# The sum over tokens with x held and k moved in 64 columns, and VectorE keeping x in plain rows

## The chip, the cores and the metric

One core of one Trainium2 chip. The metric is the device time of one execution in microseconds. TensorE (PE) multiplies, VectorE (DVE), ScalarE (ACT) and GpSimd (POOL) work element by element, SyncE (SP) issues DMAs. PEld is the loading of the operand that PE holds (the "stationary" one), which overlaps the matmuls.

## What is computed

Eight batches of 3200 tokens: a gated attention without softmax, whose result `x` goes through a token mixer.

```python
scores = (1 / S) * (z @ z.T)              # S = 3200, z is S x 64
x      = u * (maximum(scores, 0)**2 @ v)  # u, v, x are S x 256
wq, wk = x @ w_q, x @ w_k                 # S x 64
mixed  = (1 / 8) * (wq @ wk.T) @ x        # S x 256
out    = maximum(mixed, 0) @ w_out
```

The kernel never forms `wq @ wk.T`. It forms the sum over tokens `wk.T @ x`, a matrix of 64 x 256 for each batch (called heads), and multiplies `wq` with that (called mix).

## The kernel before

**Tiles and stages.** The 3200 tokens of a batch are 25 blocks of 128, in 7 groups: six of 512 tokens and a last one of 128 (`LASTG`). For each group, PE forms the scores of 128 x 512 tokens at a time (`scores`, tile `sc`, two at once as a pair on the upper and the lower 64 rows), DVE or ACT clips and scales them out of PSUM (`first_stage`, tile `g`), POOL or ACT squares them (`second_stage`, tile `at`), and some are turned by DMA for use in another group (`tt`, `ttl`). The product with `v` is accumulated in four PSUM banks (`second_product`, tiles `acc`): two halves of a group, each in two banks, one for the upper and one for the lower 64 rows of a block. All these matmuls come in pairs on the two halves of the rows, 64 rows by 128 columns.

**Behind each half of a group** (`gate`): ACT copies one bank out, DVE adds the other (tile `both`, line L369; with that the two banks are free again), and POOL multiplies by `u` and writes `x_sb` in fp16 (L388). `x_sb` is laid out in an interleaved way, so that one DMA transpose (`turn_x`) gives `xT_sb`.

**The mixer for a group.** `projections` (L417) gives q and k of the group from `xT_sb`; ACT copies them out (`qk`), a DMA transpose gives k with tokens on the partitions (`kx`, `turn_keys`), with 64 columns of k in one half of each block's 128 columns. `double_keys` (L447, POOL) copies these 64 columns into the other half, so that the 128 columns of the held operand hold k twice. `heads` (L454) then holds the doubled k (128 columns) and moves `x_sb` (256 columns), a pair for each block of 128 tokens; its result has `wk.T @ x` twice, on the upper and the lower 64 partitions, since `mix` needs it on both. `heads_out` (L467, L469, DVE) adds it to `ha`, 512 columns for the two banks, and after the last group POOL adds the two parts of `ha` to `hs` (L476). Then `mix` (L482), ACT's clip (L503), the product with `w_out` (`proj`, L513), its scaling out of PSUM by DVE or ACT (L535, L540, tile `fo` in SBUF, two buffers) and the store (L541) follow for each group of the batch.

**PSUM.** Four banks belong to `acc`. The other four are two buffers of two banks, `ps_tile`, which `sc`, `qk`, `hd`, `mx` and `fo` share in turn: a matmul into one of them waits until what stood there two tiles before has been copied out.

**Order.** The order of each engine is written out by a list scheduler in the kernel's own text. It keeps a clock for each engine (`give(engine, ready, weight)`), a list of timed calls (`at_time`), of extras that are fitted in between (`add_extra`: keys, heads, mix, proj) and of DMAs with due times (`move`), which SP issues. Engines then run in that order and wait for each other by semaphores.

**The last batch** differs: for its last three groups the sum over tokens is formed by `last_gram` and `last_heads` from a second copy of x (`xd`, L377), and the mixes stand at the end of the program, outside the scheduler.

Of the kernel before, what the change touches and what calls it, by code (L numbers as in the profile page):

```python
# [9 lines left out]
FP16 = mybir.dt.float16  # L10
# [6 lines left out]
def kernel(  # L17
# [32 lines left out]
    FINAL_SCALE = 1.0 / (8.0 * ALPHA * ALPHA * ALPHA)  # L50

    NAT = 16
    NX = 7
    NXT = 4
    NEARBY = 8
    KEEP = 4
# [3 lines left out]
    pzt = ctx.enter_context(tc.tile_pool(name="pzt", bufs=2))  # L60
    pv = ctx.enter_context(tc.tile_pool(name="pv", bufs=2))
    px = ctx.enter_context(tc.tile_pool(name="px", bufs=NX))
    pk = ctx.enter_context(tc.tile_pool(name="pk", bufs=3))
    pxt = ctx.enter_context(tc.tile_pool(name="pxt", bufs=NXT))
    pu = ctx.enter_context(tc.tile_pool(name="pu", bufs=2))
# [17 lines left out]
    def top(r):  # L83
        return slice(r * dqk, (r + 1) * dqk)

    ctx.enter_context(tc.manual_schedule())

    zT, vs, us, xs, xTs, qks, ks, hacc, hss, rts = ({} for _ in range(10))

    def rows(t, b):  # L90
        return t[b].rearrange("(p n) d -> p n d", n=NT)
# [242 lines left out]

    accs, xds = {}, {}

    def weights(b, gi, ti, j):
        if (b, gi, ti) in made:  # L340
# [20 lines left out]

    def gate(b, gi, half):
        if (b, gi) not in xs:
            assert len(xs) < NX, (b, gi, list(xs))
# [3 lines left out]
        nc.scalar.copy(out=both[:, 0 : n * D], in_=accs[half, 0][:, 0 : n * D])  # L368
        nc.vector.tensor_add(  # L369
            out=both[:, 0 : n * D], in0=accs[half, 1][:, 0 : n * D], in1=both[:, 0 : n * D]  # L370
        )
        if b == last and gi >= LASTG - 2:
            if gi == LASTG - 2 and half == 0:
                spare = pv.tile([P, NT, D], FP16, tag="v_sb", name="xd")
                for i in range(3):
                    xds[LASTG - 2 + i] = spare[:, 4 * i : min(4 * i + 4, 9), :]
            nc.vector.tensor_mul(  # L377
                out=xds[gi][:, 2 * half : 2 * half + n, :].rearrange("p n d -> p (n d)"),
                in0=both[:, 0 : n * D],
                in1=us[b, gi][:, 2 * half : 2 * half + n, :].rearrange("p n d -> p (n d)"),  # L380
            )
        u_rows = us[b, gi][:, 2 * half : 2 * half + n, :].rearrange("p n (c d) -> p (n c) d", d=dh)
        if 2 * half + n == widths[gi] // P:
            us.pop((b, gi))

        def make_x():
            for r in [half] if widths[gi] == W else range(2):
                nc.gpsimd.tensor_mul(  # L388
                    out=xs[b, gi][:, 0:n, :, r, :].rearrange("p n c d -> p (n c) d"),
                    in0=both[:, 0 : n * D].rearrange("p (m d) -> p m d", d=dh),  # L390
                    in1=u_rows,
                )

        make_x()

    def turn_x(b, gi):
# [8 lines left out]
    def x_rows(b, gi, n):  # L405
        return xs[b, gi][:, n % 2, :, n // 2, :]

    def halves(gi):  # L410
        return range((widths[gi] // P + 1) // 2)
# [30 lines left out]
    def double_keys(b, gi):  # L442
        doubled.add((b, gi))
        nn = widths[gi] // P
        for r in halves(gi):
            sl = slice(2 * r, min(2 * r + 2, nn))
            nc.gpsimd.tensor_copy(out=ks[b, gi][:, sl, r, :], in_=ks[b, gi][:, sl, 1 - r, :])  # L447

    def heads(b, gi, ps, begun=()):
        nn = widths[gi] // P  # L450
        assert (b, gi) in doubled
        for n in range(nn):
            for r in range(2):
                nc.tensor.matmul(  # L454
                    out=ps[:, r, D : 2 * D],
                    lhsT=ks[b, gi][top(r), n, :, :].rearrange("p a h -> p (a h)"),
                    rhs=x_rows(b, gi, n)[top(r), :, :],
                    start=(n == 0 and r not in begun),
                    stop=(n == nn - 1),
                )  # L460
        del xs[b, gi]

    def heads_out(b, gi, ps):
        part = ps[:, 0:2, D : 2 * D]
        if gi == 0:
            hacc[b] = psml.tile([P, 2, D], FP32, tag="ha", name="ha")
            nc.vector.tensor_copy(out=hacc[b][:], in_=part)  # L467
        else:
            nc.vector.tensor_add(out=hacc[b][:], in0=part, in1=hacc[b][:])  # L469
        if gi == LASTG:  # L470
            heads_done(b)

    def heads_done(b):
        hss[b] = psml.tile([P, D], FP16, tag="hs", name="hs")
        ha = hacc.pop(b)
        nc.gpsimd.tensor_add(out=hss[b][:], in0=ha[:, 0, :], in1=ha[:, 1, :])  # L476

    def mix(b, gi, banks):
        n = min(2, widths[gi] // P)
# [120 lines left out]
    def at_time(t, fn):  # L600
        later.append((t, fn))
# [14 lines left out]
    def add_extra(t, kind, fn):  # L616
        extras.append((t, kind, fn))
        extras.sort(key=lambda x: x[0])
# [18 lines left out]
    def close_slot(t):  # L637
        slots.append(t)
# [65 lines left out]
                row_at[b, gj, starts[gi] // P + n] = t + 0.5  # L704

    def double(b, gi):
        keys_at[b, gi] = give(POOL, clock[PE], 0.6) + 0.5
        double_keys(b, gi)

    def use_keys(b, gi):  # L710
        open_slot()
        ps = ps_tile("qk")
        prior = None
        if keyed and keys_at.get(keyed[0], 1e9) <= clock[PE]:
            prior = keyed.pop(0)
        projections(b, gi, ps, stop=not prior)
        clock[PE] += 0.44 if gi < LASTG else 0.24
        if prior:
            heads(*prior, ps, halves(gi))
            clock[PE] += 0.44 if prior[1] < LASTG else 0.11  # L720
        ready = clock[PE] + FROM_PE
        projections_out(b, gi, ps)
        done = give(ACT, ready, 0.56)
        n = widths[gi] / P
        final = (b, gi) == (last, LASTG - 2)
        if not final:
            move(
                done + SLACK, done + 10.0, 1.28, 0.21 * n, lambda: turn_keys(b, gi),
                lambda t: at_time(t, lambda: double(b, gi)),
            )  # L730
            keyed.append((b, gi))
        if prior:
            heads_out(*prior, ps)
            done = give(DVE, done, 0.7)
            if prior[1] == LASTG:
                give(POOL, done, 0.6)
                heads_known(prior[0])
        close_slot(done)
        if len(keyed) == 2 and gi == LASTG:
            add_extra(done + 14.0, "heads", use_heads)  # L740
        if final:
            for _ in keyed[1:]:
                add_extra(done, "heads", use_heads)

    def use_heads():
        open_slot()
        ps = ps_tile("hd")
        prior = keyed.pop(0)
        heads(*prior, ps)
        clock[PE] += 0.44 if prior[1] < LASTG else 0.11  # L750
        heads_out(*prior, ps)
        done = give(DVE, clock[PE] + FROM_PE, 0.7)
        if prior[1] == LASTG:
            give(POOL, done, 0.6)
            heads_known(prior[0])
        close_slot(done)

    def heads_known(b):
        t = clock[PE]
        for i, gis in enumerate(([0, 1], [2, 3, LASTG], [4, 5])):  # L760
            for gi in gis:
                add_extra(t + 4.0 + (MIXES if b < last - 1 else MIXES_END) * i, "mix", lambda gi=gi: use_mix(b, gi))

    def use_mix(b, gi):
        open_slot()
# [275 lines left out]
    while extras or later or moves:  # L1041
# [17 lines left out]
        else:  # L1059
            extras.remove(x)  # L1060
            x[2]()
    assert not pending and len(keyed) == 1
    def mixed(b, gi, i=None):
        if i is None:
            ps = ps_tile("mx")
# [22 lines left out]
    use_heads()  # L1088
# [57 lines left out]
```

## Time and profile before

| | |
|---|---|
| times of three runs | 780.02, 780.99, 781.06 us (median 780.99) |
| profiled execution | span 780.0 us |
| PE busy | 98% of the span, 12410 matmuls |
| PEld, DVE, ACT, POOL busy | 86%, 63%, 72%, 79% |
| TensorE clock granted | full in nearly every slice |
| DMA | 141 MB, 181 GB/s in the mean |

Busy time is the time in which an engine had an instruction of its own under way. A row of instructions gives line, engine, operation, what it writes and reads, the shape and the count, then busy time in us and the mean of one in ns, then the idle time before them and what ended it. A row of a timeline gives start and length in us; rows of the same kind next to each other are put together. Since matmuls overlap in the pipeline, the length of one (269 ns) is more than the distance from one to the next.

### The profile page before, as it was taken

The page shows a single profiled execution, that of the slowest core. Times are in us where ns is not written, and L with a number is a line of the kernel's source. Part 1 is how long each engine was busy: PE and PEld are TensorE (multiplying, and loading weights), DVE is VectorE, ACT ScalarE, POOL GpSimd, SP SyncE. Part 2 cuts the span into 40 slices and gives each one's busy share as a digit, 9 for nine tenths or more (in the row PEclk, how much of TensorE's full clock was granted, in tenths as well). Part 3 has the DMA queues.
Part 4 walks back from the last instruction along what each step waited for, and adds up shares of the span by engine and source line. Part 5 has one row for each costly group of instructions (what it writes and reads, how often), then busy time and mean ns, then how long its engine had stood idle before and what let it go on. Part 6 is the DMA issues. An engine that isn't in the chain of part 4 may idle for free.

```text
span 780.0 us, 28286 instructions
## 1 busy us (share of the span) xinstructions
PE 765.9 (98%) x12410; PEld 674.0 (86%) x12410; DVE 490.5 (63%) x506; ACT 558.1 (72%) x672; POOL 619.5 (79%) x518
## 2 busy tenths in 40 slices
PE   8999999999999999999999999999999999999996
PEld 6889989988888888988889888898888988999894
DVE  6576768767565766655657556575566765656534
ACT  6786785676877776876678777787778578777644
POOL 7798887668986978887779769887888868887850
PEclk9999999999999999999999999999999999999999
DMA  7899999999999999999899999999989999989725
GB/s 181 157 152 175 162 160 170 171 187 180 222 183 190 200 218 204 151 170 217 198 171 193 168 221 168 199 161 171 241 159 208 162 196 211 157 169 168 183 81 198
DMA packets 307116, 141.11 MB, mean 181 GB/s; under 512 B 285744, under 2 KB 288432, under 8 KB 306992
## 3 DMA queue, kind: packets, MB, share of 16 engines
q1 hardware_dynamic: 300224, 123.13, 85.8%
q0 software_dynamic: 6624, 15.98, 14.6%
q8 instruction: 97, 1.59, 0.9%
q14 instruction: 27, 0.22, 0.1%
q10 hardware_dynamic: 144, 0.20, 0.1%
HBM read 59.64 MB, written 26.21 MB: 110 GB/s over the span
## 4 chain that ended last, share of the span: by engine, by line
PE 94%; DVE 2%; DMA 1%; ACT 1%; issue 1%; POOL 0%; DVEq 0%; SPq 0%
PE acc L352 68%; PE sc L265 13%; PE fo L513 6%; PE qk L417 3%; PE qk L454 2%; PE mx L482 1%; DVE g L291 1%; DMA v_sb<-in_v_dram 1%; ACT g L287 1%; DVE both L369 0%; DVE fo L535 0%; DMA z<-in_z_dram 0%; ACT at L307 0%; PE xtx L555 0%; PE hd L454 0%
## 5 line engine op out<-in xcount | busy, mean ns | idle before, releaser
L352 PE MATMUL acc<-v_sb,at 64*128 64x256 f16 x7344 | 506.0, 269 | 2.3 <-issue 1.5
L309 POOL TENSOR_TENSOR at<-g 128x1024 f16<-128x1024 f32 (+2 forms) x240 | 432.5, 1813 | 88.0 <-DVE g L291 46.8
L352 PEld LDWEIGHTS <-at 64*128 64x128 f16 x7344 | 403.9, 94 | 54.5 <-issue 9.7
L291 DVE TENSOR_SCALAR g<-sc 128x1024 f32<-128x1024 f32 (+2 forms) x302 | 349.9, 1175 | 121.8 <-PE sc L265 109.8
L307 ACT ACTIVATE at<-g 128x1024 f16<-128x1024 f32 (+2 forms) x242 | 241.6, 1015 | 25.0 <-DVE g L291 22.5
L287 ACT ACTIVATE g<-sc 128x1024 f32<-128x1024 f32 (+2 forms) x177 | 174.8, 990 | 56.2 <-PE sc L265 50.9
L265 PE MATMUL sc<-zT 64*128 64x512 f16 x924 | 185.3, 375 | 2.4 <-DVE g L291 1.2
L388 POOL TENSOR_TENSOR x_sb<-both,u_sb 128x512 f16<-128x512 f32 (+1 forms) x112 | 134.3, 1205 | 48.9 <-DVE both L369 48.4
L352 PE MATMUL acc<-v_sb,tt 64*128 64x256 f16 x2272 | 168.0, 269 | 0.0
L352 PEld LDWEIGHTS <-tt 64*128 64x128 f16 x2272 | 127.0, 94 | 10.3 <-issue 0.6
L369 DVE TENSOR_TENSOR both<-acc,both 128x512 f32<-128x512 f32 (+1 forms) x104 | 69.5, 670 | 70.9 <-ACT both L368 62.0
L368 ACT COPY both<-acc 128x512 f32<-128x512 f32 (+1 forms) x104 | 58.9, 566 | 66.5 <-PE acc L352 63.1
L265 PEld LDWEIGHTS <-zT 64*128 64x128 f16 x924 | 62.2, 94 | 9.8 <-issue 5.2
L535 DVE TENSOR_SCALAR fo<-fo 128x1024 f32<-128x1024 f32 (+2 forms) x31 | 32.7, 1067 | 41.4 <-PE fo L513 41.3
L503 ACT ACTIVATE rt<-mx 128x1024 f16<-128x1024 f32 (+1 forms) x49 | 45.5, 931 | 12.2 <-PE mx L482 12.0
L430 ACT CAST qk<-qk 128x512 f16<-128x512 f32 (+1 forms) x54 | 29.4, 544 | 29.2 <-PE qk L454 25.4
L513 PE MATMUL fo<-wo,rt 128*128 128x256 f16 x400 | 49.4, 273 | 0.1
L469 DVE TENSOR_TENSOR ha<-qk,ha 128x512 f32<-128x512 f32 x37 | 25.6, 691 | 36.1 <-ACT qk L430 35.8
L513 PEld LDWEIGHTS <-rt 128*128 128x128 f16 x400 | 36.4, 98 | 10.8 <-issue 6.5
L540 ACT ACTIVATE fo<-fo 128x1024 f32<-128x1024 f32 (+2 forms) x27 | 24.6, 914 | 19.8 <-PE fo L513 19.8
L417 PE MATMUL qk<-xT_sb,wqk 64*128 64x256 f16 (+1 forms) x404 | 32.2, 265 | 0.0
L454 PE MATMUL qk<-x_sb,kx 64*128 64x256 f16 x360 | 29.1, 269 | 0.0
(44 smaller groups left out, 237.0 us busy)
## 6 DMA issues: line engine op xcount, KB each, us to landing
u_sb<-in_u_dram SPq DMA_DIRECT2D x48, 512.0 KB, 5.0
out_dram<-fo SPq DMA_DIRECT2D x46, 512.0 KB, 4.4
v_sb<-in_v_dram POOLq DMA_DIRECT2D x35, 320.0 KB, 6.2
zn<-in_z_dram POOLq DMA_DIRECT2D x7, 400.0 KB, 6.3
tt<-at SPq DMA_TRANSPOSE x143, 4.5
u_sb<-in_u_dram SPq DMA_DIRECT2D x8, 128.0 KB, 3.6
out_dram<-fo SPq DMA_DIRECT2D x8, 128.0 KB, 3.5
out_dram<-fo SPq DMA_DIRECT2D x4, 256.0 KB, 4.2
```

The costliest lines, as they stand in the source:

```text
L265: nc.tensor.matmul(out=sc[:, h, 0:gw], lhsT=z_cols(b, h, ti * P, P), rhs=z_cols(b, h, gs, gw), start=True, stop=True,)
L287: nc.scalar.activation(out=g[:, hs, 0:w], in_=sc[:, hs, 0:w], func=RELU, scale=GSCALE)
L291: nc.vector.tensor_scalar(out=g[:, hs, 0:w], in0=sc[:, hs, 0:w], scalar1=0.0, scalar2=GSCALE, op0=AOP.max, op1=AOP.mult,)
L307: nc.scalar.square(out=out, in_=g[:, hs, 0:w])
L309: nc.gpsimd.tensor_mul(out=out, in0=g[:, hs, 0:w], in1=g[:, hs, 0:w])
L352: nc.tensor.matmul(out=accs[half, r][:, ds((j % 2) * D, D)], lhsT=weights(b, gi, ti, j)[top(r), :], rhs=vs[b][top(r), ti, :], start=(first ...
L368: nc.scalar.copy(out=both[:, 0 : n * D], in_=accs[half, 0][:, 0 : n * D])
L369: nc.vector.tensor_add(out=both[:, 0 : n * D], in0=accs[half, 1][:, 0 : n * D], in1=both[:, 0 : n * D])
L388: nc.gpsimd.tensor_mul(out=xs[b, gi][:, 0:n, :, r, :].rearrange("p n c d -> p (n c) d"), in0=both[:, 0 : n * D].rearrange("p (m d) -> p m ...
L417: nc.tensor.matmul(out=ps[:, r, 0 : n * P], lhsT=wqk[top(r), c, :, :].rearrange("p t h -> p (t h)"), rhs=xTs[b, gi][top(r), 0:n, c, :], st ...
L503: nc.scalar.activation(out=out, in_=ps[:, 0:nr, 0 : ND * n * P], func=RELU)
L513: nc.tensor.matmul(out=banks[r][:, ds(j * D, D)], lhsT=flat[:, ds((dc * n + j) * P, P)], rhs=wo[:, dc, :], start=(dc == 0 and j == 0), sto ...
```

## The change

For all batches but the last, `heads` changes the two operands' places: x is held (128 of its 256 columns at a time, so twice as many matmuls) and the 64 columns of k are moved. k need not be doubled then. The result is the transposed sum, 128 partitions by 2 x 64 columns for each of two banks. `ha` has half the columns; POOL adds its two parts twice, into the two halves of a new tile `ht`, and a DMA transpose (`turn_heads`) gives `hs` in the layout that `mix` has always had. The mixes of a batch become known to the scheduler when that DMA should have landed.

A held operand must have its columns side by side. DVE therefore copies `x_sb` into a tile `xn` with plain rows (`keep_x`), once for each half of a group, after POOL has written it; the last batch's last three groups have no such copy. `x_sb` has 3 buffers in place of 7, and `xn` has 5. The last batch keeps the old operands (with `xn` moved in place of `x_sb`), and its `ha` lies in one of the two SBUF buffers with the tag `fo`.

```diff
@@ gate: after x_sb is made @@
+    def keep_x(b, gi, half):
+        if (b, gi) not in xns:
+            xns[b, gi] = pxn.tile([P, 4, D], FP16, tag="xn", name="xn")
+        n = min(2, widths[gi] // P - 2 * half)
+        nc.vector.tensor_copy(
+            out=xns[b, gi][:, 2 * half : 2 * half + n, :].rearrange("p n (c d) -> p n c d", d=dh),
+            in_=xs[b, gi][:, 0:n, :, half, :],
+        )
@@ heads @@
-        assert (b, gi) in doubled
+        x = xns.pop((b, gi))
         for n in range(nn):
-            for r in range(2):
-                nc.tensor.matmul(
-                    out=ps[:, r, D : 2 * D],
-                    lhsT=ks[b, gi][top(r), n, :, :].rearrange("p a h -> p (a h)"),
-                    rhs=x_rows(b, gi, n)[top(r), :, :],
...
+            if b == last:
+                todo = [(D, D, ks[b, gi][:, n, :, :].rearrange("p a h -> p (a h)"), x[:, n, :])]
+            else:
+                k = ks[b, gi][:, n, 1 - n // 2, :]
+                todo = [(D + c * dh, dh, x[:, n, ts(c, P)], k) for c in range(ND)]
+            for i, (at, cols, held, moved) in enumerate(todo):
+                for r in range(2):
+                    nc.tensor.matmul(
+                        out=ps[:, r, at : at + cols], lhsT=held[top(r), :], rhs=moved[top(r), :],
...
@@ heads_out @@
-            hacc[b] = psml.tile([P, 2, D], FP32, tag="ha", name="ha")
+            if b == last:
+                hacc[b] = pg.tile([P, 2, D], FP32, tag="fo", name="ha", bufs=2)
+            else:
+                hacc[b] = psml.tile([P, 2, P], FP32, tag="ha", name="ha")
@@ heads_done: POOL's sum, and the DMA that turns it @@
-        nc.gpsimd.tensor_add(out=hss[b][:], in0=ha[:, 0, :], in1=ha[:, 1, :])
+        for r in range(2):
+            nc.gpsimd.tensor_add(
+                out=hts[b][:, :, r, :],
+                in0=ha[:, 0, :].rearrange("p (c h) -> p c h", c=ND),
+                in1=ha[:, 1, :].rearrange("p (c h) -> p c h", c=ND),
+            )
+    def turn_heads(b):
+        nc.sync.dma_start_transpose(out=hss[b][:].rearrange("p (c s) -> p c s", c=ND), in_=...)
@@ scheduler @@
     def double(b, gi):
+        if b < last:
+            keys_at[b, gi] = clock[PE] + 0.5
+            return
...
+    def heads_time(b, gi):
+        t = 0.44 if b == last else 0.24
...
+            move(ready + SLACK, ready + 3.0, 1.28, 0.42, lambda: turn_heads(b),
+                 lambda t: at_time(t, lambda: heads_known(b)))
...
         gate(b, gi, half)
+        if kept_x(b, gi):
+            at_time(t, lambda: (keep_x(b, gi, half), give(DVE, t, 0.3)))
```

More of the change, by code (lines that the diff above doesn't have):

```diff
@@ L52 @@
     NAT = 16
-    NX = 7
+    NX = 3
+    NXN = 5
     NXT = 4
@@ L86 @@
     ctx.enter_context(tc.manual_schedule())
-    zT, vs, us, xs, xTs, qks, ks, hacc, hss, rts = ({} for _ in range(10))
+    zT, vs, us, xs, xns, xTs, qks, ks, hacc, hss, rts = ({} for _ in range(11))
     def rows(t, b):
@@ L394, in gate, with kept_x @@
         make_x()
+    def kept_x(b, gi):
+        return b < last or gi < LASTG - 2
+    def keep_x(b, gi, half):
+        if (b, gi) not in xns:
+            assert len(xns) < NXN, (b, gi, list(xns))
+            xns[b, gi] = pxn.tile([P, 4, D], FP16, tag="xn", name="xn")
[4 more added lines that the diff above has]
+        )
     def turn_x(b, gi):
@@ L403, in turn_x @@
         )
-    def x_rows(b, gi, n):
-        return xs[b, gi][:, n % 2, :, n // 2, :]
     def halves(gi):
@@ L450, in heads @@
         nn = widths[gi] // P
-        assert (b, gi) in doubled
+        x = xns.pop((b, gi))
         for n in range(nn):
-            for r in range(2):
-                nc.tensor.matmul(
-                    out=ps[:, r, D : 2 * D],
-                    lhsT=ks[b, gi][top(r), n, :, :].rearrange("p a h -> p (a h)"),
-                    rhs=x_rows(b, gi, n)[top(r), :, :],
[L458 to L461, printed above, removed]
+            if b == last:
+                assert (b, gi) in doubled
+                todo = [(D, D, ks[b, gi][:, n, :, :].rearrange("p a h -> p (a h)"), x[:, n, :])]
[5 more added lines that the diff above has]
+                    nc.tensor.matmul(
+                        out=ps[:, r, at : at + cols],
+                        lhsT=held[top(r), :],
+                        rhs=moved[top(r), :],
+                        start=(n == 0 and i == 0 and r not in begun),
+                        stop=(n == nn - 1 and i == len(todo) - 1),
+                    )
     def heads_out(b, gi, ps):
-        part = ps[:, 0:2, D : 2 * D]
+        cols = D if b == last else P
+        part = ps[:, 0:2, D : D + cols]
         if gi == 0:
-            hacc[b] = psml.tile([P, 2, D], FP32, tag="ha", name="ha")
+            if b == last:
+                hacc[b] = pg.tile([P, 2, D], FP32, tag="fo", name="ha", bufs=2)
+            else:
+                hacc[b] = psml.tile([P, 2, P], FP32, tag="ha", name="ha")
             nc.vector.tensor_copy(out=hacc[b][:], in_=part)
@@ L706, in double, with heads_summed @@
     def double(b, gi):
+        if b < last:
+            keys_at[b, gi] = clock[PE] + 0.5
+            return
         keys_at[b, gi] = give(POOL, clock[PE], 0.6) + 0.5
         double_keys(b, gi)
+    def heads_time(b, gi):
+        t = 0.44 if b == last else 0.24
+        return t if gi < LASTG else t / 4
+    def heads_summed(b, gi, done):
+        done = give(DVE, done, 0.7 if b == last else 0.45)
+        if gi == LASTG:
+            ready = give(POOL, done, 0.8)
+            heads_done(b)
+            move(
+                ready + SLACK, ready + 3.0, 1.28, 0.42, lambda: turn_heads(b),
+                lambda t: at_time(t, lambda: heads_known(b)),
+            )
+        return done
     def use_keys(b, gi):
@@ L733, in use_keys @@
             heads_out(*prior, ps)
[L734 to L737, printed above, removed]
+            done = heads_summed(*prior, done)
         close_slot(done)
@@ L749, in use_heads @@
         heads(*prior, ps)
-        clock[PE] += 0.44 if prior[1] < LASTG else 0.11
+        clock[PE] += heads_time(*prior)
         heads_out(*prior, ps)
[L752 to L756, printed above, removed]
+        close_slot(heads_summed(*prior, clock[PE] + FROM_PE))
     def heads_known(b):
@@ L1061 @@
             x[2]()
-    assert not pending and len(keyed) == 1
+    assert not pending and len(keyed) <= 1
     def mixed(b, gi, i=None):
```

21 lines of the change are left out of this document (13 added, 8 removed).

## The prediction

> **What bounds the kernel now.** I read the page's busy shares and its chain first, then the groups of instructions by shape, then short stretches of the timeline.
>
> ```profile
> PE 765.9 (98%) x12410; PEld 674.0 (86%) x12410; DVE 490.5 (63%) x506; ACT 558.1 (72%) x672; POOL 619.5 (79%) x518
> PE 94%; DVE 2%; DMA 1%; ACT 1%; issue 1%; POOL 0%; DVEq 0%; SPq 0%
> 299.72 2.02 PE L352 MATMUL acc<-v_sb,at 64*128 64x256 f16 x34
> ```
>
> PE is busy for 98% of the span and carries 94% of the chain that ended last. The third line shows how: 34 matmuls in 2.02 us are 17 pairs, one on the upper and one on the lower 64 rows, and with the last one's own 0.269 us taken off a pair follows the other every (2.02 - 0.27) / 16 = 0.109 us. So a pair taken off PE is worth its 0.109 us, and anything that lets PE wait costs its full length. VectorE (DVE) and GpSimd (POOL) idle for 37% and 21%, but PE's order is fixed and it has only two score buffers, so a late DVE can hold PE up without being full.
>
> **Part 1, PE: 64 columns in place of 256.**
>
> ```profile
> L454 PE MATMUL qk<-x_sb,kx 64*128 64x256 f16 x360 | 29.1, 269 | 0.0
> L454 PE MATMUL hd<-x_sb,kx 64*128 64x256 f16 x22 | 3.0, 270 | 0.0
> L417 PE MATMUL qk<-xT_sb,wqk 64*128 64x128 f16 x28 | 2.7, 216 | 0.0
> L454 PEld LDWEIGHTS <-kx 64*128 64x128 f16 x382 | 20.9, 94 | 1.3 <-issue 0.2
> 765.18 0.39 PE L417 MATMUL qq<-xT_sb,wqk 64*128 64x128 f16 x4
> 765.17 0.22 PEld L417 LDWEIGHTS <-wqk 64*128 64x128 f16 x4 [0.29 <-DMA xT_sb<-x_sb]
> ```
>
> Batches 0 to 6 have 7 x 25 = 175 token blocks, each one pair of 256 columns now (350 of the 382 matmuls): 175 x 0.109 = 19.1 us. The built program has 700 matmuls of 64 columns in their place, 350 pairs, and leaves the last batch's 32 as they are; so the change does on PE what it says. No row has 64 columns. A matmul of 128 columns takes 216 ns and one of 256 takes 269, 53 ns for 128 columns, so 192 columns fewer are 79 ns and a pair of 64 columns should follow every 0.109 - 0.079 = 0.030 us: 350 x 0.030 = 10.5 us, a gain of 8.6 us. The bounds: at half the 128-column pace the gain is the same or 1 us more; if a pair cannot come faster than the shortest spacing in the rows, (0.39 - 0.22) / 3 = 0.057 us at 128 columns, it is 20 us and the gain is gone (+0.9 us); if each pair had to wait out its weight load of 94 ns, it is 32.9 us, 13.8 us dearer. The last is unlikely: in the last row four loads of 94 ns lie within 0.22 us, so they overlap, and they did not hold the matmuls to 94 ns. I take -8.6 us, on the path, since PE is the path.
>
> The Trainium skill ("TensorE: Matmul & The Clock Gate", Back-to-back issue gap) says that starts of small matmuls never come closer than about 25 ns, whatever the column count. By that 700 matmuls would take 17.5 us and the gain would be 1.6 us; the trace has two starts for each 0.109 us pair and does not show which holds at 64 columns.
>
> **Part 2, POOL loses work.**
>
> ```profile
> L447 POOL COPY kx<-kx 128x128 f16<-128x128 f16 x92 | 24.5, 298 | 0.0
> L476 POOL TENSOR_TENSOR hs<-ha 128x256 f16<-128x256 f32 x7 | 5.1, 728 | 1.5 <-DVE ha L469 1.5
> ```
>
> Of 99 key doublings 91 go (84 x 0.298 and 7 of half size, about 26.5 us); seven sums of 0.73 us become 14 of half size, about equal. POOL falls to some 593 us. It isn't on the chain, so this is worth nothing by itself. The seven new DMA transposes of the sum stand on SP's queue among all the others; what waits for them are the mixes, which the scheduler fits in between other PE work, so I cost them at nothing in the middle batches.
>
> **Part 3, DVE's copies of x.** This is the part that decides. There are 99 new copies on DVE, each behind a wait for POOL's x_sb, with the adds that free the accumulators (L369) and the score evacuations (L291) queued behind it. DVE now reads PSUM in nearly everything it does. The few operations that read only SBUF show what happens beside POOL:
>
> ```profile
> 9.17 0.42 DVE L122 CAST zd<-z 128x512 f16<-128x512 f32 x1
> 9.50 1.26 DVE L122 CAST zd<-z 128x512 f16<-128x512 f32 x1
> L309 POOL TENSOR_TENSOR at<-g 128x512 f16<-128x512 f32 x16 | 16.7, 1056 | 1.9 <-DVE g L291 1.5 <-ACT g L287 0.3
> 9.34 1.15 POOL L309 TENSOR_TENSOR at<-g 128x512 f16<-128x512 f32 x1 [0.39 <-DVE g L291]
> 10.45 1.22 POOL L309 TENSOR_TENSOR at<-g 128x512 f16<-128x512 f32 x1
> 743.86 1.11 DVE L377 TENSOR_TENSOR xd<-both,u_sb 128x512 f16<-128x512 f32 x1
> 743.16 1.27 POOL L388 TENSOR_TENSOR x_sb<-both,u_sb 128x512 f16<-128x512 f32 x1
> 740.75 0.69 DVE L377 TENSOR_TENSOR xd<-both,u_sb 128x512 f16<-128x512 f32 x1
> ```
>
> The same cast of 512 elements takes 0.42 us when it begins ahead of POOL, and 1.26 us when it begins while POOL is at work: it ends 0.28 us behind POOL's operation (9.34 + 1.15 = 10.49). The product at 743.86 likewise takes 1.11 us against 0.69 elsewhere. So an SBUF-to-SBUF copy on DVE waits out whatever POOL is doing. The Trainium skill ("SBUF — State Buffer", Who interferes with whom) gives that as a rule, with a lock held for a whole instruction, and these rows agree; it is a rule against this change.
>
> POOL is nearly always doing something long:
>
> ```profile
> L309 POOL TENSOR_TENSOR at<-g 128x1024 f16<-128x1024 f32 x220 | 414.5, 1894 | 86.1 <-DVE g L291 45.3 <-ACT g L287 32.0 <-issue 4.0
> 300.16 1.28 POOL L388 TENSOR_TENSOR x_sb<-both,u_sb 128x512 f16<-128x512 f32 x1
> 301.39 1.90 POOL L309 TENSOR_TENSOR at<-g 128x1024 f16<-128x1024 f32 x1
> 301.88 0.69 DVE L369 TENSOR_TENSOR both<-acc,both 128x512 f32<-128x512 f32 x1 [0.67 <-ACT both L368]
> 302.75 1.22 DVE L535 TENSOR_SCALAR fo<-fo 128x1024 f32<-128x1024 f32 x1 [0.18 <-PE fo L513]
> 304.40 0.38 PE L265 MATMUL sc<-zT 64*128 64x512 f16 x2
> L139 DVE COPY zT<-ztp 128x1024 f16<-128x1024 f16 x1 | 0.7, 692 | 0.1
> ```
>
> A copy is ready the moment x_sb is (301.44). POOL has begun its next square, so the copy ends at about 303.29 + 0.15 = 303.44; L369 runs to 304.13 and not 302.57, L535 to 305.35 and not 303.97. The scores at 304.40 take the buffer that L535 frees, so PE waits 0.95 us, or 0.65 us after the 0.3 us that the scheduler of the changed kernel sets aside for a copy. The 0.15 us: the cast needs 0.28 us behind POOL and 0.42 us alone, and 16-bit data should halve its moving part of 0.27 us, as 1024 elements of 16 bits take 0.69 us in the last row and 1024 of 32 bits 1.22 us in L535's; that gives 0.15 and 0.28 us.
>
> I did this count for all 112 x_sb operations; these are the first and the last behind which PE waits:
>
> ```profile
> 27.00 1.28 POOL L388 TENSOR_TENSOR x_sb<-both,u_sb 128x512 f16<-128x512 f32 x1 [1.34 <-DVE both L369]
> 727.84 1.27 POOL L388 TENSOR_TENSOR x_sb<-both,u_sb 128x512 f16<-128x512 f32 x1
> ```
>
> The mean rest of a POOL operation at the copy is 0.84 us: nothing in 29 cases, over 1 us in 48. In 36 of the 112 PE waits, in sum 25.1 us (1.04 us at the first, 1.13 us at the last); without the 0.3 us set aside it is 39.1 us, and with copies that wait for nobody it is 0. For 99 copies I take 25.1 x 99 / 112 = 22.2 us; the ends are 0 and 35 us. POOL's own delay behind a copy (at 10.45 1.22 us, where its shape takes 1.06 us in the mean, so some 0.2 us) is paid by part 2. DVE's sums shrink from 512 to 256 columns, about 42 x 0.27 = 11 us of DVE, off the path.
>
> **Part 4, the last batch's accumulator.** `heads_out` now puts the last batch's `ha` into one of the two `fo` buffers, where it stays to the end. The built program shows three pairs of projections behind it, the first of each pair evacuated by ScalarE (ACT), the second by DVE, and both into the one buffer left. The second must wait until the first is stored.
>
> ```profile
> out_dram<-fo SPq DMA_DIRECT2D x46, 512.0 KB, 4.4
> L540 ACT ACTIVATE fo<-fo 128x1024 f32<-128x1024 f32 x22 | 22.4, 1024 | 17.5 <-PE fo L513 17.5
> L535 DVE TENSOR_SCALAR fo<-fo 128x1024 f32<-128x1024 f32 x24 | 29.2, 1224 | 39.1 <-PE fo L513 39.1
> L555 PE MATMUL xtx<-xd 128*128 128x256 f16 x18 | 2.1, 274 | 0.0
> ```
>
> From the end of the second projection: ACT's 1.02 us began 0.9 us earlier (the eight matmuls of the second projection, at the 2.1 / 18 us of the `xtx` row) and ends at +0.1; the store lands 4.4 us later, at +4.5; DVE's 1.22 us ends at +5.7. In the first two pairs PE meets the next user of that score buffer after 26 pairs and one pair of scores, 26 x 0.109 + 0.22 = 3.1 us, so it waits 2.6 us, and an estimated 1 us more if the store must queue on SP: I take 3.1 us each. The third pair stands at the end: the copy of `G`, due when `xtx` is done at +2.1, stands behind the held DVE until +5.7, 3.6 us on the tail itself. In sum 3.1 + 3.1 + 3.6 = 9.8 us; bounds 0 (the store lands early, or other waits cover it) and 14 us.
>
> **The sum** is made against the profiled execution, whose span of 780.0 us is one of the three times (780.02; median 780.99): 780.0 - 8.6 + 22.2 + 9.8 = 803.4; I say 803 us.
>
> **Rivals.**
> - *DVE's idle 37% takes up its delays* (the other side). Then copies and store wait end inside DVE's gaps and PE keeps its 8.6 us: 771.4 us. For it: L291 idles mostly for PE, so DVE is often ahead. Against it: the gaps lie in the wrong place at 301.88 to 304.40. It decides as faster when PE's new waits in sum stay under 8.6 us, which is a copy of about 0.5 us in the mean and a short wait at the store.
> - *Only one of the two waits reaches PE*: 780.0 - 8.6 + 9.8 = 781.2 us with the buffer alone, 793.6 us with the copies alone.
> - *Pairs of 64 columns come no faster than those of 128*: +0.9 in place of -8.6, 813 us, and 826 us at the weight load's 94 ns. Nothing in the rows forces it, nothing excludes it. The Trainium skill's 25 ns (the page and section named above) would make it milder: a gain of 1.6 us and 810 us.
>
> **How the numbers follow.** Forecast 0.60 (its own range 789 to 819 us, from 10 to 35 us of copies), DVE's idle time 0.20, one wait alone 0.10 (0.04 within 0.2% of now, 0.06 slower), slow short pairs 0.10. About 0.2%, 1.6 us, is what a measurement can tell from no change. Faster 0.20, same 0.04, slower 0.76. The range 773 to 822 us leaves out the lower part of the first rival and the upper part of the last.
>
> **What would show it.** Copies `xn` with a mean near 1.0 us and a wide spread (0.3 to 2.1) bear out part 3; a mean under 0.45 us refutes it. PE's idle time, now almost none, should grow by some 30 us, put down to DVE's L291 and L369 (as they are numbered now), and `fo` on DVE should wait for a store three times for several us in the last 40 us. Matmuls with `xn` held should show pairs every 0.03 us. Fewer than 10 us of new PE waits would make the prediction wrong, as would a shorter span with copies that do wait: then PE's order has more slack than I counted.

## The result

The changed kernel takes 807.4 us in the median (805.7 to 810.7) against 780.5 us for the kernel before: a ratio of 1.034, 95% interval 1.031 to 1.037. It is 27 us slower; the forecast was 803 us. One execution in a slower state, of 809.9 us in run 12, is left out of that run's median and ratio.

**The profile after.** Its profiled execution has a span of 808.6 us, 28.6 us more than before. First the page: busy shares, the granted clock in 40 slices, and the chain that ended last.

```profile
PE 771.8 (95%) x12760; PEld 680.8 (84%) x12760; DVE 536.0 (66%) x594; ACT 571.0 (71%) x683; POOL 600.0 (74%) x434
PEclk9999999999999999999999999999999999999897
PE 79%; DVE 7%; ACT 5%; issue 4%; DMA 3%; POOL 2%; SPq 0%; POOLq 0%; DVEq 0%; ACTq 0%
```

PE now idles for 36.8 us (before: 14.1), its share of the chain has fallen from 94% to 79%, and DVE, at 66%, carries 7% of a chain in which it had 2%. DVE did not become full; it became late. The groups of the new operations, by shape, and the distribution of the copies (count, shortest/median/longest in ns):

```profile
L405 DVE COPY xn<-x_sb 128x512 f16<-128x512 f16 x92 | 75.8, 835 | 0.8 <-POOL x_sb L389 0.4
L472 PE MATMUL qk<-kx,xn 64*128 64x64 f16 x648 | 18.9, 190 | 0.0
465.50 0.41 PE L472 MATMUL qk<-kx,xn 64*128 64x64 f16 x16
L405 DVE COPY xn<-x_sb x99: 217/458/3261, 29.6 to 750.1; 128x512 f16<-128x512 f16 x92, 128x256 f16<-128x256 f16 x7
```

The 16 matmuls of the third row are 8 pairs: (0.41 - 0.19) / 7 = 0.031 us from pair to pair, where 256 columns took 0.109. The large copies vary by a factor of 12 at one size (0.28 to 3.26 us; the 217 ns are of the small form). That is the mark of waiting inside the instruction. Their wait is not in the idle column (0.8 us): it is in the busy time, 75.8 us, of which 92 x 0.283 = 26 us would do if none waited (0.283 us is the median of those 14 beside which GpSimd was idle).

The waits (engine and line, for whom: us in total, times, longest), and a stretch of the timeline in which one copy leads to a wait of PE:

```profile
DVE fo L566 <- DMA out_dram<-fo: 21.0, 3, 9.5
PE sc L267 <- DVE g L293: 8.7, 15, 2.5
PE sc L267 <- DVE fo L566: 6.3, 1, 6.3
PEld hl L596 <- DVE G L1130: 3.8, 1, 3.8
```

```profile
710.69 1.95 POOL L311 TENSOR_TENSOR at<-g 128x1024 f16<-128x1024 f32 x1
710.80 1.98 DVE L405 COPY xn<-x_sb 128x512 f16<-128x512 f16 x1
712.71 3.47 DVE L293 TENSOR_SCALAR g<-sc 128x1024 f32<-128x1024 f32 x3
713.97 0.39 PE L267 MATMUL sc<-zT 64*128 64x512 f16 x2 [2.45 <-DVE g L293]
```

POOL begins its square at 710.69, the copy comes 0.11 us later and ends at 712.78, 0.14 us behind the square. The score evacuation that stood behind it is late, and PE waits 2.45 us for the buffer. A gap, from here on, is what the distance from one start of a matmul to the next has over the time that its columns take (half of the 0.109 us of a pair, for 256). PE has about 42 us of gaps in this trace and about 11 in that of before, 31.3 us more. The 350 short pairs, at 0.0317 us in the mean of the 20 groups of 16 that stand undivided in the trace, take 11.1 us in place of 19.1, 8.0 us saved. That makes -8.0 + 31.3 = +23.3 us. The 5.3 us that are left of the 28.6 are a remainder that fits the clock: it is at half speed in three stretches, 20.5 us in sum (the 8 and the 7 in the line of the clock are the two longer ones, the third is too short to show in tenths), and PE is busy for 15.4 us of them.

### The profile page after: what moved, and what is told of

It is laid out like the page before. It is cut to its first block, busy times and chain, and to the rows that moved or that the text cites. A ratio compares the mean times of both kernels' runs of the same rounds, so it can differ in the third digit from the quotient of the medians.

```text
span 808.6 us, 28956 instructions
## 1 busy us (share of the span) xinstructions
PE 771.8 (95%) x12760; PEld 680.8 (84%) x12760; DVE 536.0 (66%) x594; ACT 571.0 (71%) x683; POOL 600.0 (74%) x434
## 4 chain that ended last, share of the span: by engine, by line
PE 79%; DVE 7%; ACT 5%; issue 4%; DMA 3%; POOL 2%; SPq 0%; POOLq 0%; DVEq 0%; ACTq 0%
PE acc L354 59%; PE sc L267 10%; PE fo L544 5%; DVE g L293 3%; ACT g L289 2%; PE qk L428 2%; ACT at L309 1%; PE mx L513 1%; DVE xn L405 1%; POOL at L311 1%; DMA out_dram<-fo 1%; PE qk L472 1%; DMA v_sb<-in_v_dram 1%; DVE both L370 1%; ACT both L369 1%
## 5 line engine op out<-in xcount | busy, mean ns | idle before, releaser
L354 PE MATMUL acc<-v_sb,at 64*128 64x256 f16 x7344 | 513.0, 270 | 4.9 <-DVE both L370 2.0
L354 PEld LDWEIGHTS <-at 64*128 64x128 f16 x7344 | 409.4, 94 | 51.6 <-issue 17.6
L293 DVE TENSOR_SCALAR g<-sc 128x1024 f32<-128x1024 f32 (+2 forms) x290 | 336.7, 1177 | 108.5 <-PE sc L267 102.7
L289 ACT ACTIVATE g<-sc 128x1024 f32<-128x1024 f32 (+1 forms) x189 | 185.6, 985 | 62.7 <-PE sc L267 54.6
L354 PE MATMUL acc<-v_sb,tt 64*128 64x256 f16 x2272 | 176.6, 270 | 0.0
L354 PEld LDWEIGHTS <-tt 64*128 64x128 f16 x2272 | 131.4, 94 | 9.0 <-issue 0.6
L405 DVE COPY xn<-x_sb 128x512 f16<-128x512 f16 (+1 forms) x99 | 79.9, 816 | 0.8 <-POOL x_sb L389 0.4
L490 DVE TENSOR_TENSOR ha<-qk,ha 128x256 f32<-128x256 f32 (+1 forms) x37 | 16.2, 437 | 27.4 <-ACT qk L441 27.4
```

The source lines that it names most:

```text
L289: nc.scalar.activation(out=g[:, hs, 0:w], in_=sc[:, hs, 0:w], func=RELU, scale=GSCALE)
L293: nc.vector.tensor_scalar(out=g[:, hs, 0:w], in0=sc[:, hs, 0:w], scalar1=0.0, scalar2=GSCALE, op0=AOP.max, op1=AOP.mult,)
L354: nc.tensor.matmul(out=accs[half, r][:, ds((j % 2) * D, D)], lhsT=weights(b, gi, ti, j)[top(r), :], rhs=vs[b][top(r), ti, :], start=(first ...
L405: nc.vector.tensor_copy(out=xns[b, gi][:, 2 * half : 2 * half + n, :].rearrange("p n (c d) -> p n c d", d=dh), in_=xs[b, gi][:, 0:n, :, ha ...
```

## The experiments

The theory was the prediction's: three terms that add (matmuls -8.6, copies +22.2, buffer +9.8). Its rivals: that DVE takes up the copies, or that something else is behind the loss. Each comparison is with the kernel before on the same chip. Runs 1 to 4, 5 to 8 and 9 to 12 were taken on three chips, on which the kernel before took 780.5, 780.8 and 780.3 us (780.8 beside run 12), so a difference between runs of two groups carries some 0.5 us from that. Times are medians; the ratios, with 95% intervals, are estimated from all runs kept and can differ a little from those of the medians.

**1. Without the copies (e1_no_copies).** One constant tile in place of all `xn`; the order is otherwise that of the kernel after, 0.3 us for each copy still set aside.

```diff
+    xn_once = pxn.tile([P, 4, D], FP16, tag="xn", name="xn")
+    nc.gpsimd.memset(xn_once[:], 0.5)
-            xns[b, gi] = pxn.tile([P, 4, D], FP16, tag="xn", name="xn")
+            xns[b, gi] = xn_once
-        nc.vector.tensor_copy(out=xns[b, gi]..., in_=xs[b, gi]...)
```

> The changed kernel without its 99 copies of x: xn is one tile filled once at the start, so the sum over tokens is taken of constants; the order of PE, ACT and DVE is otherwise the same, and the scheduler still sets aside 0.3 us for each copy. Theory (the copies wait out POOL's operation and hold up what stands behind them on DVE): PE's stalls outside the last batch go, about 18 us, and the time is 787 to 791 us. Rival (DVE's idle time takes up the copies, the loss lies in the short matmuls and their weight loads): within 3 us of the changed kernel, 804 us or more.

799.6 us (ratio 1.025, 1.017 to 1.033): between the two that were expected. Only about 8 us come back, so the copies are not 22 us in this order.

**2. The last batch's sum in a buffer of its own (e2_own_ha).** The order of every engine stays as it was.

```diff
-                hacc[b] = pg.tile([P, 2, D], FP32, tag="fo", name="ha", bufs=2)
+                hacc[b] = pz.tile([P, 2, D], FP32, tag="zn", name="ha")
```

> The changed kernel with the last batch's accumulator in the buffer of z's plain rows (free by then), so that both fo buffers serve the stores; the order of every engine is the same. Theory (three evacuations wait for a store to land): they start at once, PE's stall of 6.5 us at 750 us and the wait of 3.7 us for G go, and with them the half clock behind them, some 5 us: 790 to 796 us. Rival (the stores are covered, the last batch is late for other reasons): 803 us or more.

794.4 us (1.015, 1.011 to 1.020), so the buffer costs 13.0 us. Stretches of the two kernels near the end show why it is more than the waits (start:end, length, busy us and matmuls of PE, then of PEld, DVE, ACT and POOL; the clock granted is the third number from the end):

```profile
745.00:756.00 11.00, 5.95 (x56) 4.59 (x57) 3.45 (x5) 2.05 (x2) 1.89 (x1) 0.53 0.41 131
789.00:797.00 8.00, 6.62 (x40) 4.13 (x40) 3.22 (x6) 2.74 (x7) 0.00 (x0) 0.57 0.16 66
```

```profile
745.00:756.00 11.00, 11.00 (x192) 9.14 (x190) 7.26 (x8) 7.72 (x11) 10.00 (x8) 1.00 0.48 145
756.00:789.00 33.00, 31.01 (x406) 24.93 (x402) 16.02 (x22) 17.45 (x31) 10.42 (x10) 1.00 0.51 160
```

The first fence is the kernel after, with the stretches of its two waits. The second is this run: the first stretch again, and what follows it nearly to the end of the span of 793.3 us. From 745 to 756 us PE has 56 matmuls with the shared buffer and 192 without, and the clock is at half in nearly all of it. Without the shared buffer it is full from 745 to 789 us.

**3. Both at once (e3_no_copies_own_ha).**

The edits of 1 and 2 together.

> Both edits: no copies (xn one constant tile, so the sum over tokens is of constants) and the accumulator in a buffer of its own. What is left of the change is the held x, the moved k of 64 columns and the turned sum. Theory (the two waits are the whole loss, and pairs of 64 columns come every 0.03 us): 771 to 773 us. Rival (pairs of 64 columns come no faster than those of 128, or the longer way of the sum by DMA delays the mixes): 779 us or more.

785.8 us (1.006, 1.004 to 1.009). Here the theory falls: with both waits gone the kernel should have been at 772, and it is slower than before. 13 to 14 us are neither the copies nor the buffer. PE's gaps are about 20 us in place of 11, many of them small ones of 0.3 to 0.6 us, and PE's busy time is 763.5 us, only 2.4 less than before. A third suspect remains: the order. The change alters the durations and due times that the scheduler counts with, and by that the sequence on every engine.

**4. Copies with an odd count of blocks (e4_odd_copies).** The copy of 8 blocks of 64 columns, as 3 and 5.

```diff
-        nc.vector.tensor_copy(out=..., in_=...)
+        for sl in (slice(0, 3), slice(3, 4 * n)):
+            nc.vector.tensor_copy(out=dst[:, sl, :], in_=src[:, sl, :])
```

> The changed kernel with each copy made as two, of 3 and of 5 (last group 1) blocks of 64 columns. In the kernel before a cast of 7 blocks of 64 took 0.62 us beside POOL's work, as one element a cycle gives, while those of 4 and 8 blocks waited for POOL. Theory (a copy waits for POOL because it reads two elements a cycle or more by the port that POOL uses): copies of an odd number of blocks run at one element a cycle, 0.3 and 0.45 us, end without regard to POOL, and the time is 788 to 794 us, although DVE works longer. Rival (what counts is DVE's time and its wait for x_sb, not POOL's port): twice the copies cost more, 810 us or more.

796.8 us (1.020, 1.014 to 1.025): 10.6 us below the kernel after, with twice as many copies, but 2.8 us above the 788 to 794 expected and far below the rival's 810. The pieces don't wait, and they are faster than expected: 0.243 and 0.308 us in the mean, not 0.3 and 0.45.

**5. The operand swap alone, in the old order (e5_old_order).** As 3, with the scheduler's durations and due times put back, and POOL writing the halves straight to `hs` (the turn by DMA is left out).

```diff
-        t = 0.44 if b == last else 0.24
-        return t if gi < LASTG else t / 4
+        return 0.44 if gi < LASTG else 0.11
...
-            move(ready + SLACK, ready + 3.0, 1.28, 0.42, lambda: turn_heads(b), ...)
+            heads_known(b)
-                add_extra(t + 0.5 + (MIXES ...
+                add_extra(t + 4.0 + (MIXES ...
```

> The kernel after with four things put back or left out: no copies of x (the sums read one constant tile), the last batch's sum in a buffer of its own, the scheduler's assumed durations and due times as in the kernel before, and the halves added on GpSimd straight into the factor of the mix (the turn by DMA is left out, so the output is not the reference's). What is left of the change is the operand swap: x held, k moved in 64 columns. Every engine then has its instructions in the order of the kernel before. Theory (the matmuls give their 8.6 us, and the run without copies and buffer at 785.8 lost them to the order that the scheduler wrote with the changed durations): 771 to 774 us, with TensorE's waits on DVE g and DVE both as in the kernel before (2.5 and 1.4 us). Rival (the swap itself brings the waits, or the short pairs don't save): 779 us or more, waits as in that run.

772.5 us (0.991, 0.988 to 0.993): 8.3 us below before. Page and waits:

```profile
PE 758.5 (98%) x12760; PEld 669.4 (87%) x12760; DVE 477.3 (62%) x506; ACT 557.5 (72%) x672; POOL 600.2 (78%) x435
PE sc L267 <- DVE g L293: 1.2, 5, 0.4
```

PE is busy 7.4 us less than before and waits no more than before. So the short pairs are worth what they were forecast at. DVE and ACT have the instructions of the kernel before here, in its order. Run 3 differs from this run in the order and in the turn by DMA, and PE nowhere waits for the DMA of `hs` in run 3; so the order is what is left to explain the 13.3 us that it lost, and run 8 tests whether an order alone can cost as much. Of the two profiled executions run 3's is 10.0 us longer, and the gaps explain 9.4 of that. Which of the altered durations and due times makes the order dear was not tested.

Runs 6, 7 and 10 leave the turn out as well. Their times say what the copies cost; they are not times of the whole change.

**6. The copies in the old order (e6_old_order_copies).**

```diff
+        nc.vector.tensor_copy(out=xns[b, gi]..., in_=xs[b, gi]...)   # to run 5; NX = 2, NXN = 6
```

> As e5_old_order, but with the real copies of x on VectorE (one more x buffer in plain rows, one less in the interleaved order). Theory (the copies wait for GpSimd's operations and hold up VectorE): 8 to 12 us over e5_old_order, some 780 to 785. The prediction's own price of 22 us would give about 794. Rival (in this order VectorE's idle time takes them): within 2 us of e5_old_order.

796.2 us (1.020, 1.018 to 1.023): 23.7 us over run 5. The expectation of 8 to 12 us, taken from runs 1 to 3, is wrong. The prediction's 22.2 us is near, but it isn't the prediction's figure for this order: nothing is set aside for the copies here, and its count without the 0.3 us is 39.1 us, for 99 copies 39.1 x 99 / 112 = 34.6 us.

```profile
L405 DVE COPY xn<-x_sb 128x512 f16<-128x512 f16 x92 | 88.0, 958 | 0.2 <-POOL x_sb L389 0.2
PE sc L267 <- DVE g L293: 14.0, 22, 1.9
```

PE's gaps rise from about 11 to about 35 us, which is the whole loss. In an order that knows nothing of the copies they cost 23.7 us. In that of the kernel after, with 0.3 us set aside for each, run 2 less run 3 gives 8.6 us, but that order costs 785.8 - 772.5 = 13.3 us by itself.

**7. The odd copies in the old order (e7_old_order_odd).** The edit of 4 made to run 6.

> As e6_old_order_copies, with each copy issued as two, of 3 and 5 blocks of 64 columns. Theory (copies in this shape do not wait for GpSimd, and the 55 us of added VectorE work lie in its idle time): 1 to 5 us over e5_old_order, some 773 to 778, the fastest form of this change that is left. Rival (the added work alone is the cost): as e6_old_order_copies or slower, 780 or more.

772.9 us (0.991, 0.989 to 0.994): 0.3 us over run 5, less than can be told from nothing, though DVE works 37 us more.

```profile
L408 DVE COPY xn<-x_sb 128x320 f16<-128x320 f16 x92 | 28.4, 308 | 0.0
L408 DVE COPY xn<-x_sb 128x192 f16<-128x192 f16 x99 | 24.0, 243 | 1.4 <-POOL x_sb L389 1.4
L408 DVE COPY xn<-x_sb 128x64 f16<-128x64 f16 x7 | 2.3, 330 | 0.0
PE sc L267 <- DVE g L293: 2.0, 6, 0.4
```

It is the wait that costs, not the work: 320 columns take 0.308 us, more than 512 take without a wait in one piece (0.283 us), and cost PE nothing. None of the pieces of 3 and 5 blocks takes over 0.32 us. The seven pieces of one block are no example of it: the longest takes 1.26 us, where 0.17 us will do, and ends 0.04 us behind a square of POOL.

**8. A new order alone (e8_before_late_mix).** The kernel before, with one due time of the scheduler moved.

```diff
-                add_extra(t + 4.0 + (MIXES if b < last - 1 else MIXES_END) * i, "mix", ...)
+                add_extra(t + 8.0 + (MIXES if b < last - 1 else MIXES_END) * i, "mix", ...)
```

> The kernel before with one number of the scheduler changed: the mixes of a batch are due 4 us later (t + 8.0 for t + 4.0). All work is the same and the result too; a third of the rows in the order of each engine move. Theory (a new order alone costs several us, since the old one was chosen for its timing): 784 to 790 us, with new waits of 0.3 to 0.6 us on DVE g and DVE both. Rival (orders of this scheduler are worth the same, and the loss is the swap's own): 780 to 782 us.

789.7 us (1.011, 1.009 to 1.012): the same matmuls, sums and stores, 8.9 us slower.

```profile
PE sc L265 <- DVE g L291: 3.4, 7, 1.1
PE acc L352 <- DVE both L369: 2.0, 6, 0.5
```

Before, these two were 1.2 us (5 times) and 0.2 us (once). A due time is a price.

**9. The whole change without its two waits (e9_odd_own_ha).** Runs 2 and 4 together.

> The kernel after, whole, with both waits taken away: each copy as 3 and 5 blocks of 64 columns, the last batch's sum in a buffer of its own; the order is that of the kernel after. Theory (the costs of the copies and of the buffer add, and what stays is the order that the scheduler wrote): 796.8 less the 13.0 us of the buffer, 781 to 787. Rival (the two waits hide behind each other, or the order costs nothing): below 778 or above 792.

783.9 us (1.004, 1.003 to 1.005). The two costs add: 796.8 - 13.0 = 783.8. What is left over run 7 is 11.1 us, the new order with the turn; PE does not wait for the DMA of `hs` here either.

**10. An even split (e10_even_split).** As 7, with 4 and 4 blocks.

```diff
-        for sl in (slice(0, 3), slice(3, 4 * n)):
+        for sl in (slice(0, 2 * n), slice(2 * n, 4 * n)):
```

> As e7_old_order_odd, but with each copy split 4 and 4 blocks in place of 3 and 5: the same count of instructions, the same bytes, an even count of blocks. Theory (a copy with an even count of blocks waits for GpSimd's operation, one with an odd count does not): both halves wait, so as e6_old_order_copies or slower, 793 us or more. Rival (it is the splitting, shorter pieces fit between, that took the wait away): 773 to 777 as e7_old_order_odd.

824.6 us (1.057, 1.053 to 1.061): 51.8 us over run 7 with the same bytes in as many copies.

```profile
L408 DVE COPY xn<-x_sb 128x256 f16<-128x256 f16 x184 | 128.2, 738 | 0.2 <-POOL x_sb L389 0.2
PE sc L267 <- DVE g L293: 34.3, 32, 2.2
```

Of the 92 pairs of large pieces the first piece waits in 65 and the second in 26, and 14 of the second ones take over 1.9 us, as long as a whole square of POOL; a pair takes 1.48 us in the mean, where the copy in one piece takes 0.96. So not every piece waits, as the expectation had it, but enough do. Not the length of a piece decides, but the shape: 256 columns wait, 192 and 320 don't. The Trainium skill ("VectorE: DVE Perf Modes", Mode 2×_2P) has a copy use both read ports when its outermost dimension is even, or odd and equal on both sides, and ("SBUF — State Buffer", Who interferes with whom) has only such a copy share a port pair with GpSimd under a lock. That agrees with 8 and 4 blocks waiting and 3 and 5 not, given that the written side, plain rows, is one run of columns (320 for a read side of 5 blocks of 64) and so not equal to 3 or 5. A piece of one block is a run of 64 columns on both sides, and it waits.

**11. A better order for the whole change (e11_retuned).** Run 9 with four constants of the scheduler changed.

```diff
-    MIXES = 18.0
+    MIXES = 16
-    XDUE = 5.0
-    XWAIT = 7.0
-    LATE = 0.3
+    XDUE = 4
+    XWAIT = 6
+    LATE = 0.2
```

> As e9_odd_own_ha, whole, with four constants of the scheduler changed (MIXES 16, XDUE 4, XWAIT 6, LATE 0.2), so that its plan ends 12.9 us earlier by its own count (763.9 for 776.8; the plan of the kernel before ends at 764.4). Theory (what was left over the kernel before in e9_odd_own_ha was the order): about 13 us below e9_odd_own_ha, 769 to 776, faster than the kernel before. Rival (the plan's count says nothing of the chip, the order isn't the cause): 781 or more.

778.2 us (0.9965, 0.9945 to 0.9986): 5.7 us below run 9, less than half of the 12.9 us by which the scheduler's clock for PE stood earlier at the end of its plan; the time lies between the theory and the rival. It is the whole change, and 0.35% faster than the kernel before. That the order was part of the loss is borne out; that the plan's own count gives the time is not.

**12. The whole change in the old order (e12_old_order_turn).** Run 7 with the DMA turn put in, issued when POOL's adds should be done.

```diff
+            at_time(ready, lambda: turn_heads(b))   # to run 7, hs turned from ht
```

> As e7_old_order_odd, but whole: the sum goes through its tile ht and the DMA turn, which is issued once GpSimd's adds should be done; TensorE, VectorE and ScalarE keep the order of e7_old_order_odd. There the first mix of each batch follows GpSimd's second add after 0.25 to 2.47 us (sum over seven batches 9.7 us), and the turn takes 4.5 us from issue to landing. Theory (the turn does not fit into the old order, so this change needs a new one): seven waits of TensorE for the DMA hs, in sum 7 x 4.5 - 9.7 = 21.8 us, so 790 to 800 us. Rival (the turn is hidden, the old order would have done): 773 to 777.

801.4 us in the median of three (794.2, 801.4 and 805.5; 1.023, 1.011 to 1.036).

```profile
PEld L513 <- DMA hs<-ht: 21.6, 7, 8.2
DMA to landing us min/median/max: 2.3/3.2/4.9
```

The second line is of the seven turns. The seven waits are there, and the median is above the 790 to 800 forecast; the clock granted was at half for 20.5 us of this trace. That their sum of 21.6 us meets the 21.8 expected is in part luck: the turns landed 3.2 us after issue in the median and not 4.5, and the longest wait, 8.2 us, holds 3.7 us in which the first turn had not been issued. The turn does not fit into the old order as it stands, so the whole change needs another one. How dear that must be is open: the order of the kernel after costs 11.1 us over run 7 (run 9), that of run 11 5.4 us.

**The account**, each step a difference of two medians. It closes by construction, and with intervals of 2 to 4 us on each run the third step can't be told from nothing:

| step | us |
|---|---|
| operand swap (before to 5) | -8.3 |
| copies, old order (5 to 6) | +23.7 |
| new order that knows of them, with the turn (6 to 2) | -1.8 |
| the buffer (2 to after) | +13.0 |
| sum from 780.8 | 807.4 |

## Why the prediction was right, and where it was not

The total was met, 803 for 807.4 us, and so was the main mechanism, copies that wait for POOL and hold PE up. The total is partly luck: Part 3 was too dear by more than half and a term of about that size was missing.

**Part 1, -8.6 us: right.** Pairs every 0.031 us for 0.030 forecast; run 5 gives -8.3 us. The rival of slow pairs is out, and with it the milder one that the prediction takes from the Trainium skill, 25 ns from start to start. A pair's 31.7 ns hold two starts, so one of every two follows within 16 ns, and the measurement differs from that floor. The trace of before showed it already: with 256 columns the starts follow each other by 20 and 89 ns in turn.

**Part 2, nothing: wrong in one sentence.** POOL's lost work is worth nothing that can be seen: run 5's -8.3 us holds it too. But the turn of the sum was costed at nothing because "the scheduler fits in" the mixes. Run 12 shows that in the old order it brings 21.6 us of waits. In the order that the scheduler wrote for the change PE does not wait for it, but that order has a cost of its own: 13.3 us without copies (5 to 3), 11.1 us with odd ones (7 to 9). The prediction has no term for it.

**Part 3, +22.2 us: the mechanism right, the size met by luck.** In the kernel after, copies and order together are 794.4 - 772.5 = 21.9 us, but 13.3 of these are the order and only 8.6 the copies, which were forecast at 22.2. The count was made in the places of the old order. For that order its own figure is 34.6 us (run 6), and 23.7 were measured, so the count is too dear by 11 us there too. Taking the 0.3 us set aside off each wait counted the benefit of the new order as a discount; in fact the new order takes most of the copies' cost away and brings more of another kind. Its rule, that a copy from SBUF to SBUF waits out whatever POOL is doing, is too wide: pieces of 8, 4 and 1 blocks wait, pieces of 3 and 5 don't (runs 7 and 10). The copies that wait end 0.15 us behind POOL in the median, as forecast. Their mean is 0.84 us in place of 1.0 for the large ones, and four were far longer than one operation of POOL: this is such a pair of copies.

```profile
307.51 1.89 POOL L311 TENSOR_TENSOR at<-g 128x1024 f16<-128x1024 f32 x1
308.38 3.64 DVE L405 COPY xn<-x_sb 128x512 f16<-128x512 f16 x2
309.35 0.59 POOL L154 DMA_DIRECT2D v_sb<-in_v_dram  x1
309.96 1.91 POOL L311 TENSOR_TENSOR at<-g 128x1024 f16<-128x1024 f32 x1
```

**Part 4, +9.8 us: the mechanism right, the size too small by 3.2 us.** DVE's `fo` waits three times for a store, 21.0 us in sum, but one of the three costs PE nothing (3.1 forecast), one 6.3 us (3.1 forecast) and the one on the tail 3.8 us (3.6 forecast). That 6.3 and 0 make nearly 3.1 and 3.1 is luck. The 2.9 us that are left of the 13.0 fit the clock, a term that was missing: at these two waits it is at half for 10.2 and 6.8 us (the first fence of run 2). How much of the 13.0 us is the clock's was not measured by itself.

**The rivals.** DVE's idle 37% does not absorb the copies: run 6 has 22 waits of PE for DVE with DVE 30% idle. It absorbs the work once it doesn't wait (run 7). "Only one wait reaches PE" is out by runs 2 and 4.

**The signs given.** PE's idle time grew by 22.7 us of the span and by 31.3 us from start to start; the forecast was 30. The waits for DVE's `g` and `both`, at which it was to show, are 8.7 and 2.0 us of that. The copies' mean was over 0.45 us, their spread 0.2 to 3.3. The three waits for a store end at 748.8, 771.9 and 788.8 us, so within the last 70 us and not 40. The prediction's own range, 789 to 819 us for 10 to 35 us of copies, does not follow from its terms, which give 791 to 816.

## What to carry to other kernels

Ask of each operation that is added to DVE not how long it takes but what it may wait for inside itself: here 99 copies in pieces of 8 blocks cost 23.7 us and the same bytes as 3 and 5 blocks 0.3 us. In a kernel whose order is planned, a duration or due time that is touched writes a new order, and that alone was worth 9 to 13 us in three comparisons here, more than the matmuls that were saved; measure an edit once in the old order and once in the new, and look for a new order before the edit is judged. A result that must be turned by DMA needs a place in the plan: here 2.3 to 4.9 us from issue to landing, and the time until it is issued.

## What was not expected of the hardware

- **Half clock behind a wait.** After PE's wait of 2.45 us at 713.97 the granted clock is at half from 714.8 to 718.2, and 3.4, 6.8 or 10.2 us were the lengths of all such stretches ahead of the end of a run. The Trainium skill ("TensorE: Matmul & The Clock Gate", What's actually happening) tells of half clock after an idle window of about 3.4 us: the length agrees, but here shorter waits did it. The length of the wait does not decide alone. In run 6 a wait of 2.17 us at 359.46 brought half clock and a longer one of 2.42 us at 209.03 did not (the clock is again the third number from the end):

```profile
209.00:215.00 6.00, 5.87 (x111) 5.37 (x112) 3.67 (x6) 5.80 (x8) 2.18 (x2) 1.00 0.80 171
359.00:365.00 6.00, 5.54 (x68) 4.84 (x69) 3.02 (x5) 3.30 (x4) 1.89 (x1) 0.72 1.16 270
```

In all traces 7 of the 12 idle times of PE of 2.0 to 2.5 us, the start of the program aside, were followed by half clock; one of 3.5 us (run 4, at 784.46) was not. What decides is open. At half clock for 3.4 us, such a wait can cost up to 1.7 us more than itself.
- **A copy can lose twice.** Four copies of the kernel after took 2.5 to 3.3 us; in the stretch shown above two took 3.64 us, while POOL ended a square, issued a DMA for 0.59 us and began the next square. That the issue of the DMA itself holds DVE up is a reading of that stretch and was not tested.
